# Attention, a mixture of experts and a softplus layer on one core: a staggered front of twelve attention steps, four slots for each later step, and a softplus remainder one slot later

## The chip, the cores and the metric

The kernel runs on one core of one Trainium2 chip. The metric is the device time of one execution in microseconds, the median of some runs. The matmuls are TensorE's (PE in the rows); VectorE (DVE), ScalarE (ACT) and GpSimd (POOL) work beside it, each on its own queue in order, and SyncE (SP) issues most transfers.

## What is computed

```python
# attention: 4 batches, 8 heads, 576 queries, head dimension 64; keys and values are averaged over 8
k_p = k.reshape(B, H, Sp, pool, D).mean(axis=3)
v_p = v.reshape(B, H, Sp, pool, D).mean(axis=3)
scores = scale * np.matmul(q, k_p.transpose(0, 1, 3, 2))
attn = softmax(scores)                       # exp of the scores minus their maximum, over the sum + 1e-9
x = matmul(attn, v_p)                        # as 2304 rows of 512
# mixture of 8 experts, 512 -> 1024 -> 512
P = exp(x @ w_gate - max); 8 times: rows to sum 1, columns to sum 1, times N / E
for e in range(E):
    out += P[:, e:e + 1] * (np.maximum(x @ w1[e], 0.0) @ w2[e])
# softplus layer, 512 -> 2048 -> 512
h = out @ w_in
g = np.maximum(h, 0.0) + np.log1p(np.exp(-np.abs(h)))
y = g @ w_out
```

## The kernel before, in words

**Products.** The 2304 rows are three thirds of 768. A phase is one layer over one third: three phases of experts, then three of softplus (`phases`). A phase has units of 256 hidden columns, 32 in an expert phase and 8 in a softplus phase, 120 in all. Each operand of a product is a rounded part hi and a remainder lo, and a product is three matmuls (`three`, L524). The first product of a unit (`first`, L553) is a Strassen form with seven block products of 6 matmuls, 128x384 each, 42 in all; its inputs are four blocks of x and sums of them (t1 to t4, `t_sums`), each as hi and lo (`splits`), and four sums of the weights (`sums_w1`, L170, and `prep_w1`, L181). The second product (`second`, L600) takes 6 row tiles of 6 matmuls 128x512, 36 in all, and DVE adds each result from its PSUM bank py onto an accumulator g. The order of work is `todo`: first 0, first 1, second 0, first 2, second 1 and so on. After the first product, `pending` holds four activations. `relu` (L540) or `softplus` (L547) writes h as hi on ACT and as lo on DVE; one of them follows the first product and the others follow the row tiles of the second product before.

**Attention.** It has 32 steps of one pair of heads and 288 queries (`attn_step`, L396). A step turns its queries (`channels_first`, bank pq, copied by ACT), computes the scores (`softmax`, L308, bank s), takes the maximum and the difference on DVE into an SBUF tile ex, exp on ACT, sum and reciprocal on DVE and the product on POOL (`divide`, L326), then six transposes (`turn_attn`, bank pa, copied by ACT to aT) and the mix with V (`mix`, bank px, copied by ACT into x or xb). Each fourth step is followed by `gate` (bank pg). Keys and values of a pair of heads are used by eight steps over two halves of the queries. In the front the keys are summed by 16 matmuls with the identity (`keys_first`, bank pk) and the values by three additions on POOL; later two reductions on DVE do it (`pool_kv`, L255) and one transpose.

The first 14 steps (`AHEAD`) run ahead of all products, the front. Then the sums and parts of x for the first third are made (L807 to L817). The other 18 steps run inside the products: `hook` (L749) is called at some 13 slots of a unit, 7 in its first product and 6 in its second, and every fifth slot runs one whole step. When attention has ended, the slots work off the list `side` (the gate's normalisation, the shares of the experts whose sums were kept raw, `shares_to_raw`), and later the conversion of the softplus weights from 64-bit floats (`from_float64`) and the preparation of the next phase's x (`turn`, `t_sums_banked`, `remainders`). Before expert 4 of the first phase `flush` runs what is left in the list at once (L880); the shares of the fourth expert are put there just before (L895).

**PSUM.** While attention runs, all eight banks are one pool. Then they are four for the first product (p), three for py and the side work's banks (xs, xh, pt), and one for the conversion (c).

The order on each engine is the order in which the code is written (`manual_schedule`); tiles wait for the release of the buffer that they take.

## Time and profile before

| | us |
|---|---|
| median of 3 runs (2056.94 to 2063.78) | 2063.13 |
| the profiled execution | 2063.6 |
| its span in the profile | 2061.8 |

| engine | busy us | share | instructions |
|---|---|---|---|
| PE (matmul) | 2010.8 | 98% | 10643 |
| DVE | 1364.5 | 66% | 2417 |
| POOL | 1258.2 | 61% | 1069 |
| ACT | 822.5 | 40% | 1607 |

Matmuls overlap in a pipeline, so their busy time counts some time twice and hides short gaps; the pace of matmuls that follow each other (start to start) tells more. A row of the timeline shows in brackets how long the engine was idle before it and what ended that. PEclk is the granted clock of TensorE as a share of 2.4 GHz; its other level is 1.2 GHz.

### The profile page before, as it was taken

Reading aid. Unit: us, or ns where it says so; the run is one execution under the profiler, and the core shown is the slowest. Engines: PE = TensorE matmul, PEld = TensorE weight load, DVE = VectorE, ACT = ScalarE, POOL = GpSimd, SP = SyncE. Lnnn points to the kernel's source line nnn. Section 1 sums busy time; section 2 is a strip of 40 time slices with the busy share of each in tenths; the row PEclk is TensorE's granted clock in tenths of the full one; section 3 lists DMA queues with packets and bytes.
Section 4 is the critical chain, followed back from the end, with each engine's and each line's share of the span. In section 5 each row is a group of like instructions: output and inputs, shape, how many; then the busy total and the mean of one; then the engine's idle time right before and its main releaser. Section 6 shows DMA issues by size and latency. Waiting matters only on the chain.

```text
span 2061.8 us, 28361 instructions
## 1 busy us (share of the span) xinstructions
PE 2010.8 (98%) x10643; PEld 1788.7 (87%) x10643; DVE 1364.5 (66%) x2417; ACT 822.5 (40%) x1607; POOL 1258.2 (61%) x1069
## 2 busy tenths in 40 slices
PE   8898999999999999999999999999999999999999
PEld 6677889889989988988899898989989998888998
DVE  3677558777666677677777677666777546546455
ACT  3453544323433333433233423333322455654543
POOL 5554556666566567557666666665676555655653
PEclk8799999999999999999999999999999999999999
DMA  6242122223234234323322432233333323433421
GB/s 167 74 122 80 61 75 62 82 92 118 85 114 126 81 92 134 94 92 102 103 98 92 152 113 96 87 89 98 92 103 102 104 79 96 144 93 110 160 63 62
DMA packets 142311, 205.70 MB, mean 100 GB/s; under 512 B 27916, under 2 KB 88796, under 8 KB 142172
## 3 DMA queue, kind: packets, MB, share of 16 engines
q1 hardware_dynamic: 132092, 190.12, 30.1%
q10 hardware_dynamic: 10080, 13.77, 1.8%
q8 instruction: 83, 1.36, 0.3%
q14 instruction: 56, 0.46, 0.1%
HBM read 173.76 MB, written 30.09 MB: 99 GB/s over the span
## 4 chain that ended last, share of the span: by engine, by line
PE 83%; DVE 5%; POOL 5%; ACT 3%; issue 3%; DMA 1%; SPq 0%; ACTq 0%; DVEq 0%; POOLq 0%
PE py L527 41%; PE p L527 37%; POOL w1lo L165 2%; PE s L314 1%; ACT w1hi L194 1%; PE px L352 1%; POOL w2lo L165 1%; PE pk L297 1%; POOL sums L165 1%; PE pa L342 1%; DMA f<-in_moe_w_out_dram 1%; DVE p L569 1%; DVE za L569 0%; PE pq L283 0%; DMA f<-in_moe_w_in_dram 0%
## 5 line engine op out<-in xcount | busy, mean ns | idle before, releaser
L527 PE MATMUL py<-w2hi,hhi 128*128 128x512 f32 x1440 | 565.9, 393 | 15.7 <-DVE g L614 8.9
L165 POOL TENSOR_TENSOR w1lo<-w1raw,w1hi 128x512 fp32r<-128x512 f32 x240 | 241.8, 1029 | 556.1 <-ACT w1hi L194 556.1
L527 PE MATMUL p<-xhi,w1hi 128*128 128x384 f32 x1680 | 568.2, 338 | 10.2 <-DVE p L569 4.6
L527 PE MATMUL p<-xlo,w1hi 128*128 128x384 f32 x1680 | 564.8, 336 | 3.6 <-DVE xlo L479 3.6
L527 PE MATMUL p<-xhi,w1lo 128*128 128x384 f32 x1680 | 565.1, 336 | 3.0 <-POOL w1lo L165 3.0
L527 PE MATMUL py<-w2hi,hlo 128*128 128x512 f32 x1440 | 565.8, 393 | 0.0
L527 PE MATMUL py<-w2lo,hhi 128*128 128x512 f32 x1440 | 565.1, 392 | 0.0
L629 DVE SCALAR_TENSOR_TENSOR g<-py,prob,g 128x512 f32<-128x512 f32 x468 | 349.7, 747 | 94.8 <-PE py L527 83.5
L527 PEld LDWEIGHTS p<-xhi,w1hi 128*128 128x128 f32 x1680 | 316.6, 188 | 28.2 <-DVE p L569 7.5
L527 PEld LDWEIGHTS py<-w2hi,hhi 128*128 128x128 f32 x1440 | 271.1, 188 | 78.4 <-DVE g L614 12.8
L542 ACT ACTIVATE hhi<-p 128x384 fp32r<-128x384 f32 x384 | 180.5, 493 | 391.2 <-PE p L527 347.6
L527 PEld LDWEIGHTS p<-xlo,w1hi 128*128 128x128 f32 x1680 | 316.6, 188 | 14.2 <-DVE xlo L479 4.4
L527 PEld LDWEIGHTS py<-w2hi,hlo 128*128 128x128 f32 x1440 | 270.8, 188 | 57.6
L527 PEld LDWEIGHTS p<-xhi,w1lo 128*128 128x128 f32 x1680 | 316.4, 188 | 3.6 <-POOL w1lo L165 3.6
L527 PEld LDWEIGHTS py<-w2lo,hhi 128*128 128x128 f32 x1440 | 270.9, 188 | 49.0
L165 POOL TENSOR_TENSOR w2lo<-w2raw,w2hi 128x1024 fp32r<-128x1024 f32 x120 | 289.5, 2412 | 14.8 <-ACT w2hi L202 14.8
L165 POOL TENSOR_TENSOR w1lo<-sums,w1hi 128x1024 fp32r<-128x1024 f32 x120 | 289.4, 2411 | 0.0
L571 ACT COPY za<-p 128x384 f32<-128x384 f32 x120 | 57.5, 479 | 538.7 <-PE p L527 538.7
L543 DVE SCALAR_TENSOR_TENSOR hlo<-p,hhi 128x384 fp32r<-128x384 f32 x384 | 210.4, 548 | 28.8 <-ACT hhi L542 28.7
L569 DVE TENSOR_TENSOR za<-p,za 128x384 f32<-128x384 f32 x120 | 66.8, 556 | 215.4 <-PE p L527 215.4
L569 DVE TENSOR_TENSOR u<-p,za 128x384 f32<-128x384 f32 x120 | 66.8, 556 | 126.4 <-PE p L527 92.5
L202 ACT CAST w2hi<-w2raw 128x1024 fp32r<-128x1024 f32 x120 | 126.5, 1054 | 0.0
(111 smaller groups left out, 2015.3 us busy)
## 6 DMA issues: line engine op xcount, KB each, us to landing
w1raw<-in_moe_w_dram SPq DMA_DIRECT2D x96, 512.0 KB
w2raw<-in_moe_w_dram SPq DMA_DIRECT2D x96, 512.0 KB
xlod<-xl ACTq DMA_DIRECT2D x70, 192.0 KB
xlo<-xlod SPq DMA_DIRECT2D x35, 384.0 KB
w1raw<-v SPq DMA_DIRECT2D x24, 512.0 KB
w2raw<-v SPq DMA_DIRECT2D x24, 512.0 KB
f<-in_moe_w_in_dram SPq DMA_DIRECT2D x16, 512.0 KB
v<-dt SPq DMA_DIRECT2D x32, 256.0 KB
```

Source lines behind the costliest of these rows:

```text
L165: nc.gpsimd.tensor_tensor(o, a, b, op=ALU.subtract)
L194: nc.scalar.copy(at(hi), src)
L202: nc.scalar.copy(hi, raw)
L297: nc.tensor.matmul(pk[h * D:(h + 1) * D, :SP], kt[:, h, t, :], ident[:SP, :SP], start=t == 0, stop=t == POOL - 1,)
L314: nc.tensor.matmul(ps[:QP, j * 2 * SP:(j + 1) * 2 * SP], qT[:, j * QP:(j + 1) * QP], kb)
L342: nc.tensor.transpose(pa[:SP, j * QP:(j + 1) * QP], ex[:, 2 * j + h, :], ident[:QP, :QP])
L527: nc.tensor.matmul(ps, lhs[a], rhs[b], start=first and i == 0, stop=last and i == 2, skip_group_check=goes_on,)
L542: nc.scalar.activation(hh, src, AF.Relu)
L543: nc.vector.scalar_tensor_tensor(hl, src, 0.0, hh.bitcast(F32), op0=ALU.max, op1=ALU.subtract)
L569: add = lambda o, x, y: nc.vector.tensor_tensor(o, x, y, op=ALU.add)
L571: nc.scalar.copy(a, pa)
L629: nc.vector.scalar_tensor_tensor(a, py, prob[:, t, e:e + 1], a, op0=ALU.mult, op1=ALU.add)
```

## The change

- **The front** is a loop of 12 steps and two more passes in which each part of a step has its own iteration: `front(k)` runs the scores of step k, the transposes of step k - 2, the queries of step k + 1, exp of step k, the keys for later, the division of step k - 1 and the mix of step k - 2. In these steps the difference and exp are written back into the scores' bank, and the division's product is DVE's, from the bank into ex. The keys' bank is copied by ACT (before: DVE). Values are summed on POOL always.
- **x of the first third**: `mix` also writes hi and lo of b11, b21 and b22 from the bank px (ACT and DVE); t1 to t4 are summed and split in halves inside the front's last iterations, partly on POOL. Unit 0's first product begins inside the last two passes (block products m1 and a12), and units 0 and 1 have their weights prepared inside the front.
- **Each later step** has four slots: queries and scores; exp, the transposes of the step before, the first half of a key reduction; division and values; mix and the second half of the key reduction.
- **The shares of the fourth expert** are put into the list behind the flush.
- **Softplus**: the remainder of each activation is DVE's one entry of `pending` later. In the last phases `turn`, xs and xh take the bank c instead of a py bank.
- `load_kv` loads K and V apart; the numbers in `keys_summed` and `values` load pairs 6 and 7 of both twice.

```diff
+    AHEAD = 12
...
-    AHEAD = 14
...
+    def values(i):
+
+        vt = v_t.pop(i)
         vp = at_p.tile([SP, 2, D], F32, tag="vp", name="vp", bufs=NK + 1)
-        early = pooled_at[i] < AHEAD
-        kp = None
-        if not early:
-            kp = at_p.tile([SP, 2, D], F32, tag="kp", name="kp", bufs=1)
-            nc.vector.tensor_reduce(kp, kt.rearrange("p h t d -> p h d t"), axis=AX.X, op=ALU.add)
-        if early:
-            pool_add(vt[:, :, 0:4, :], vt[:, :, 0:4, :], vt[:, :, 4:8, :])
-            pool_add(vt[:, :, 0:2, :], vt[:, :, 0:2, :], vt[:, :, 2:4, :])
-            pool_add(vp, vt[:, :, 0, :], vt[:, :, 1, :])
-        else:
-            nc.vector.tensor_reduce(vp, vt.rearrange("p h t d -> p h d t"), axis=AX.X, op=ALU.add)
-        pooled[i] = kp, vp
-        if early:
-            keys_first(i, kt)
-
-        if pool is ld_p or next_kv[0] < 2 * HP:
-            load_kv(pool)
+        pool_add(vt[:, :, 0:4, :], vt[:, :, 0:4, :], vt[:, :, 4:8, :])
+        pool_add(vt[:, :, 0:2, :], vt[:, :, 0:2, :], vt[:, :, 2:4, :])
+        pool_add(vp, vt[:, :, 0, :], vt[:, :, 1, :])
+        vp_t[i] = vp
+        load_kv(i + (4 if i < 4 else 2), v_t)
...
+        keys_out(i, pk, lambda o, a, s: nc.scalar.activation(o, a, AF.Copy, scale=s))
+        load_kv(i + (4 if i < 4 else 2), k_t)
...
+    def keys_reduced(i, h):
+
+        if h == 0:
+            kp_t[i] = at_p.tile([SP, 2, D], F32, tag="kp", name="kp", bufs=1)
+        nc.vector.tensor_reduce(
+            kp_t[i][:, h], k_t[i][:, h].rearrange("p t d -> p d t"), axis=AX.X, op=ALU.add
+        )
+        if h:
+            del k_t[i]
+            load_kv(i + 2, k_t)
...
+        ev = sv if early else turned()
         nc.vector.tensor_reduce(mx, sv, axis=AX.X, op=ALU.max)
-        nc.vector.tensor_tensor(ex, sv, mx.unsqueeze(2).to_broadcast([QP, G, SP]), op=ALU.subtract)
+        nc.vector.tensor_tensor(ev, sv, wide(mx), op=ALU.subtract)
         def exp():
-            nc.scalar.activation(ex, ex, AF.Exp)
+            nc.scalar.activation(ev, ev, AF.Exp)
         def divide():
             sm = at_p.tile([QP, G], F32, tag="sm", name="sm")
-            nc.vector.tensor_reduce(s1, ex, axis=AX.X, op=ALU.add)
+            ex = turned() if early else ev
+            nc.vector.tensor_reduce(s1, ev, axis=AX.X, op=ALU.add)
             nc.vector.tensor_scalar_add(s1, s1, 1e-9)
             nc.vector.reciprocal(sm, s1)
-            nc.gpsimd.tensor_tensor(ex, ex, sm.unsqueeze(2).to_broadcast([QP, G, SP]), op=ALU.mult)
+            (nc.vector if early else nc.gpsimd).tensor_tensor(ex, ev, wide(sm), op=ALU.mult)
             to_turn.append((m, ex))
-        return exp, divide
+        to_exp.append(exp)
+        to_divide.append(divide)
...
+        if here:
+            tb = TP0 // 2
+            for j in range(2):
+                a, z = max(t0, j * tb), min(t0 + here, (j + 1) * tb)
+                if a < z and (hp // 2, j) in first_x:
+                    hi, lo = (t[:, hp % 2, a - j * tb:z - j * tb] for t in first_x[hp // 2, j])
+                    src = px[:, a - t0:z - t0]
+                    nc.scalar.activation(hi, src, AF.Copy, scale=1.0 / POOL)
+                    nc.vector.scalar_tensor_tensor(
+                        lo, src, 1.0 / POOL, hi.bitcast(F32), op0=ALU.mult, op1=ALU.subtract
+                    )
...
+    keys_at = {-1: (0,), 0: (1,), 1: (2,), 2: (3,), 4: (4,), 5: (5,), 6: (6,), 7: (7,)}
+    pooled_at = {8: 12, 9: 13, 10: 14, 11: 15, 12: 18, 13: 21, 14: 22, 15: 23}
...
+    def attention():
+        for m in range(AHEAD, STEPS + 2):
+            now = [i for i in pooled_at if pooled_at[i] == m]
+            while to_gate:
+                gate()
+            if m + 1 < STEPS:
+                channels_first(m + 1)
+            if m < STEPS:
+                softmax(m)
+            yield
+            while to_exp:
+                to_exp.pop(0)()
+            while to_turn:
+                turn_attn()
+            for i in pooled_at:
+                if pooled_at[i] == m - 1:
+                    keys_turned(i)
+            for i in now:
+                keys_reduced(i, 0)
+            yield
+            while to_divide:
+                to_divide.pop(0)()
+            for i in now:
+                values(i)
+            yield
+            while to_mix:
+                mix()
+            for i in now:
+                keys_reduced(i, 1)
+            yield
+    def front(k):
+        if k < AHEAD:
+            softmax(k)
+        if to_turn:
+            turn_attn()
+        if k + 1 <= AHEAD:
+            channels_first(k + 1)
+        while to_exp:
+            to_exp.pop(0)()
+        for i in keys_at.get(k, ()):
+            keys_summed(i)
+        while to_divide and (len(to_divide) > 1 or k >= AHEAD):
+            to_divide.pop(0)()
         while to_gate:
             gate()
+        if to_mix:
             mix()
...
-                    got.append(bank("xs")[:, :a.shape[2]])
+                    got.append(bank("xs", spare[0])[:, :a.shape[2]])
...
-        nc.vector.tensor_tensor(hl, src, hh.bitcast(F32), op=ALU.subtract)
+        return lambda: nc.vector.tensor_tensor(hl, src, hh.bitcast(F32), op=ALU.subtract)
...
+            tail = [None]
+            for x, i, j in order:
+                def act(x=x, i=i, j=j):
+                    if tail[0]:
+                        tail[0]()
+                    tail[0] = softplus(at(i, j), ps(x))
+                pending.append(act)
+            pending.append(lambda: tail[0]())
...
+    def first(n, between, done=None):
+        do = done or first_parts(n)
+        order = ("s1", "s2", "a22", "s3") if done else ("m1", "s2", "s1", "a22", "s3", "a12")
+        for k, x in enumerate(order):
+            do[x]()
+            between(k)
...
-        if attn_m[0] is not None:
-            if slot[0] % 5 == 2:
-                attn_step(attn_m[0], False)
-                attn_m[0] += 1
-                if attn_m[0] >= STEPS and not to_turn and not to_mix and not to_gate:
-                    attn_m[0] = None
-                    finish_attention()
+        if attn[0] is not None:
+            if next(attn[0], 0) == 0:
+                attn[0] = None
+                finish_attention()
...
+    def t_half(eng, i, a, b):
+        return lambda c: eng.tensor_tensor(t0_of(i)[:, c], a(c), b(c), op=ALU.subtract)
+    def t_split(eng, name, i, c):
+        if c == 0:
+            xs_next[name] = [xpool.tile([P, 2, TP0 // 2], F32R, tag="x", name=f"x{n}") for n in ("hi", "lo")]
+        hi, lo = (t[:, c] for t in xs_next[name])
+        nc.scalar.copy(hi, t0_of(i)[:, c])
+        eng.tensor_tensor(lo, t0_of(i)[:, c], hi.bitcast(F32), op=ALU.subtract)
+    x0_sum = {
+        1: t_half(nc.gpsimd, 0, on_b(0, 1), on_b(0, 0)),
+        3: t_half(nc.gpsimd, 2, on_b(1, 1), on_b(0, 1)),
+        2: t_half(nc.vector, 1, on_b(1, 1), on_t(0)),
+        4: t_half(nc.vector, 3, on_b(1, 0), on_t(1)),
+    }
+    xs_next.update({"b11": first_x[0, 0], "b21": first_x[1, 0], "b22": first_x[1, 1]})
...
+    for it in range(AHEAD + 2):
+        if it == AHEAD:
+            xs.update(xs_next)
+            unit0 = first_parts(0)
+            unit0["m1"]()
+        if it == AHEAD + 1:
+            unit0["a12"]()
+        front(it)
+        if it in (0, 1, 2, 3, 4, 5):
+            values(it)
+        if it == 2:
+            load_w(2, 0)
+        if it == 4:
             sums_w1(0)
+            parts[0] = w1_parts(0)
+        if it in (5, 6):
+            next(parts[0])
+        if it == 7:
+            values(6)
+            next(parts[0])
+            next(parts[0], None)
             load_w(1, 1)
+        if it == 8:
+            values(7)
+            ta = hpool.tile([P, 2, 2, TP0 // 2], F32, tag="hhi", name="ta")
+            tb = hpool.tile([P, 2, 2, TP0 // 2], F32, tag="hlo", name="tb")
+            t0_of = lambda i: (ta, tb)[i // 2][:, i % 2]
+        if it == 9:
+            sums_w1(1)
+        if it == 10:
+            parts[1] = w1_parts(1)
+            x0_sum[1](0)
+            t_split(nc.gpsimd, "t1", 0, 0)
+        if it == 11:
+            x0_sum[1](1)
+            t_split(nc.gpsimd, "t1", 0, 1)
+            next(parts[1])
+            next(parts[1])
+        if it in (12, 13):
+            c = it - 12
+            x0_sum[2](c)
+            t_split(nc.vector, "t2", 1, c)
+            x0_sum[3](c)
+            x0_sum[4](c)
+            t_split(nc.gpsimd, "t4", 3, c)
+            t_split(nc.vector, "t3", 2, c)
+    next(parts[1])
+    next(parts[1], None)
+    load_w(1, 2)
...
                 flush()
+                shares_to_raw([RAW - 1])
...
-            if f == 0 and u == RAW * UPE - 1:
-                shares_to_raw([RAW - 1])
...
             if f == 2 and u == NU1 - 1:
                 assert converting[0] is None
+                spare[0] = "c"
```

How instructions move, at three places. On DVE in the front, one step before and one after (mx: the maximum; s<-ex and s<-s: the sum; kbd: the keys):

```order
L320 TENSOR_REDUCE mx<-s 96x6
L321 TENSOR_TENSOR ex<-s,mx 96x432
L302 TENSOR_SCALAR kbd_129<-pk 64x72 x2
L328 TENSOR_REDUCE s<-ex 96x6
L329 TENSOR_SCALAR s<-s 96x6
L330 RECIPROCAL sm<-s 96x6
```

```order
L337 TENSOR_REDUCE mx<-s 96x6
L338 TENSOR_TENSOR s<-s,mx 96x432
L346 TENSOR_REDUCE s<-s 96x6
L347 TENSOR_SCALAR s<-s 96x6
L348 RECIPROCAL sm<-s 96x6
L349 TENSOR_TENSOR ex<-s,sm 96x432
L390 SCALAR_TENSOR_TENSOR xlo<-px,xhi 128x288
```

The keys' copy has left DVE; the product ex and a remainder of x from px have come.

On POOL behind the front, where the first products run (sums and w1lo: weights of the first product, w2lo: of the second, ex: the product of the division, vt and vp: the sums of V), before:

```order
L331 TENSOR_TENSOR ex<-ex,sm 96x432 x3
L165 TENSOR_TENSOR w1lo<-w1raw,w1hi 128x512
L165 TENSOR_TENSOR w1lo<-w1raw,w1hi 128x256
L165 TENSOR_TENSOR w1lo<-sums,w1hi 128x1024
L165 TENSOR_TENSOR w2lo<-w2raw,w2hi 128x1024
```

and after:

```order
L886 TENSOR_TENSOR xlo<-tb,xhi 128x384
L165 TENSOR_TENSOR w1lo<-sums,w1hi 128x1024
L349 TENSOR_TENSOR ex<-ex,sm 96x432
L162 TENSOR_TENSOR vt<-vt 72x2x256
L162 TENSOR_TENSOR vt<-vt 72x2x128
L162 TENSOR_TENSOR vp<-vt 72x128
L165 TENSOR_TENSOR w2lo<-w2raw,w2hi 128x1024
```

The sums of V, which were reductions on DVE here, now stand between a step's product and the remainder of the second product's weights.

On DVE in a softplus phase, from the first block sum of a unit on (u, za and the p tiles: block sums, g: the addition from py), before:

```order
L569 TENSOR_TENSOR p_16850<-p_16850,za 128x384
L551 TENSOR_TENSOR hlo<-p_16847,hhi 128x384
L614 TENSOR_TENSOR g_2974<-py,g_2974 128x512
L569 TENSOR_TENSOR p_16849<-p_16849,u_16852 128x384
L551 TENSOR_TENSOR hlo<-p_16848,hhi 128x384
```

and after:

```order
L632 TENSOR_TENSOR pd<-pd,za 128x384
L702 TENSOR_TENSOR g_2931<-py,g_2931 128x512
L632 TENSOR_TENSOR pc<-pc,u_16876 128x384
L608 TENSOR_TENSOR hlo<-pa,hhi 128x384
L702 TENSOR_TENSOR g_2931<-py,g_2931 128x512
```

The first addition from py now stands ahead of the first remainder, and each remainder is one addition later.

## Rows read from the trace of the kernel before

**Rows 1.** Chain of waits in order of time: start us, us, what.

```profile
345.02 6.84 PE py L527 x30
351.86 6.26 PE p L527 x36
```

**Rows 2.** Busy time by stretch, tile p on PE: length, busy (count), PEclk, DMA.

```profile
0.00:88.50 88.50, 3.16 (x7) 0.79 0.52 137
88.50:300.00 211.50, 82.29 (x413) 0.98 0.28 81
```

**Rows 3.** The same view for tile py.

```profile
88.50:300.00 211.50, 77.17 (x310) 0.98 0.28 81
```

**Rows 4.** Chain of waits in the front, one iteration.

```profile
34.58 0.96 PE pa L342 x6
35.54 2.12 PE pk L297 x32
37.66 0.96 PE px L352 x4
38.62 0.67 PE pq L283 x3
39.29 1.44 PE s L314 x6
```

**Rows 5.** Busy time of PE in one stretch of the front, PEclk and DMA share.

```profile
26.80:88.50 61.70, 50.16 (x463) 0.69 0.38 99
```

**Rows 6.** Timeline of PE: start us, us, instructions [idle before <-releaser].

```profile
53.53 0.69 PE L342 MATMUL pa<-ident,ex 96*72 96x96 f32 x6 [3.12 <-POOL ex L331]
```

**Rows 7.** Timeline of DVE, one softmax of the front.

```profile
50.44 0.60 DVE L320 TENSOR_REDUCE mx<-s 96x6 f32<-96x432 f32 x1 [0.19 <-PE s L314]
51.15 0.60 DVE L321 TENSOR_TENSOR ex<-s,mx 96x432 f32<-96x432 f32 x1
...
52.51 0.19 DVE L330 RECIPROCAL sm<-s 96x6 f32<-96x6 f32 x1
```

**Rows 8.** Groups of instructions on POOL: count | busy us, mean ns | idle before.

```profile
L165 POOL TENSOR_TENSOR w2lo<-w2raw,w2hi 128x1024 fp32r<-128x1024 f32 x120 | 289.5, 2412 | 14.8 <-ACT w2hi L202 14.8
...
L331 POOL TENSOR_TENSOR ex<-ex,sm 96x432 f32<-96x432 f32 x32 | 29.7, 930 | 96.7 <-DVE sm L330 55.6 <-ACT w1hi L194 19.5 <-PE p L527 8.4
...
L162 POOL TENSOR_TENSOR vt<-vt 72x512 f32<-72x512 f32 (+1 forms) x20 | 19.9, 994 | 8.6 <-DMA vt<-in_v_dram 7.8
```

**Rows 9.** Timeline of DVE and PE at the first products.

```profile
82.31 3.42 DVE L479 TENSOR_TENSOR xlo<-g,xhi 128x768 fp32r<-128x768 f32 x1
...
85.79 0.69 PE L527 MATMUL p<-xlo,w1hi 128*128 128x384 f32 x1 [3.28 <-DVE xlo L479]
```

**Rows 10.** Timeline of PE and DVE; last, busy time of all engines in one stretch, PEclk.

```profile
108.66 0.65 PE L527 MATMUL p<-xhi,w1lo 128*128 128x384 f32 x1 [1.70 <-POOL w1lo L165]
...
163.20 1.92 DVE L268 TENSOR_REDUCE vp<-vt 72x128 f32<-72x1024 f32 x1
...
166.24 0.44 PE L527 MATMUL p<-xhi,w1hi 128*128 128x384 f32 x1 [3.07 <-DVE p L569]
...
160.00:170.00 10.00, 6.93 (x28) 5.87 (x27) 8.28 (x12) 4.75 (x9) 7.00 (x5) 0.84 0.55 171
```

**Rows 11.** Timeline of DVE and PE at the flush.

```profile
417.18 0.74 DVE L782 SCALAR_TENSOR_TENSOR g<-g,prob,g 128x512 f32<-128x512 f32 x1
...
422.43 5.29 DVE L782 SCALAR_TENSOR_TENSOR g<-g,prob,g 128x512 f32<-128x512 f32 x3
...
428.44 0.50 PE L527 MATMUL py<-w2hi,hhi 128*128 128x512 f32 x1 [2.47 <-DVE g L629]
```

**Rows 12.** Waits of PE in total (us, times, longest), and DVE's timeline.

```profile
PE py L527 <- DVE g L614: 8.9, 8, 1.6
...
PE py L527 <- DVE g L467: 2.3, 2, 1.1
...
1736.46 0.56 DVE L551 TENSOR_TENSOR hlo<-p,hhi 128x384 fp32r<-128x384 f32 x1 [1.03 <-ACT hhi L550]
```

More of the change, by code (lines that the diff above doesn't have):

```diff
@@ L566, in first, with ps @@
         tb = PAIRS[sets[n][2]] // 2
-        pa, pb, pc, pd = (bank(f"p{x}", "p")[:, :tb] for x in "1654")
+        got = {}
+        def ps(x):
+            if x not in got:
+                got[x] = bank(f"p{x}", "p")[:, :tb]
+            return got[x]
         a, u1 = (zpool.tile([P, tb], F32, tag="z", name=x) for x in ("za", "u1"))
         add = lambda o, x, y: nc.vector.tensor_tensor(o, x, y, op=ALU.add)
-        product(pa, A11, "b11")
-        nc.scalar.copy(a, pa)
-        between(0)
-        product(pb, S2, "t2")
@@ L574, in first @@
-        add(u1, pb, a)
-        between(1)
-        product(pc, S1, "t1")
-        between(2)
-        product(pd, A22, "t4")
-        between(3)
-        product(pb, S3, "t3", True)
-        add(a, pb, a)
-        add(pb, pc, a)
-        add(pd, pd, a)
-        between(4)
-        product(pa, A12, "b21", True)
-        between(5)
-        def rest():
-            product(pc, S4, "b22", True)
-            add(pc, pc, u1)
-        between(6)
-        act = relu if sets[n][1] == "moe" else softplus
@@ L594, in first, with m1, s2, s1 @@
-        pending.extend([
-            lambda: act(at(0, 0), pa), lambda: act(at(1, 1), pb),
-            lambda: act(at(1, 0), pd), lambda: act(at(0, 1), pc),
-        ])
-        return rest
+        def m1():
+            product(ps("a"), A11, "b11")
+            nc.scalar.copy(a, ps("a"))
+        def s2():
+            product(ps("b"), S2, "t2")
+            add(u1, ps("b"), a)
+        def s1():
+            product(ps("c"), S1, "t1")
+        def a22():
+            product(ps("d"), A22, "t4")
@@ new lines, in s3, with a12, s4, out @@
+        def s3():
+            product(ps("b"), S3, "t3", True)
+            add(a, ps("b"), a)
+            add(ps("b"), ps("c"), a)
+            add(ps("d"), ps("d"), a)
+        def a12():
+            product(ps("a"), A12, "b21", True)
+        def s4():
+            product(ps("c"), S4, "b22", True)
+            add(ps("c"), ps("c"), u1)
+        def out():
+            order = (("a", 0, 0), ("b", 1, 1), ("d", 1, 0), ("c", 0, 1))
+            if sets[n][1] == "moe":
+                pending.extend([lambda x=x, i=i, j=j: relu(at(i, j), ps(x)) for x, i, j in order])
+                return
+            tail = [None]
[6 more added lines that the diff above has]
+            pending.append(lambda: tail[0]())
@@ L861, in between @@
                 hook()
-            rest = first(n, between)
+            rest = first(n, between, None if n else unit0)
             pending.pop(0)()
```

193 lines of the change are left out of this document (86 added, 107 removed).

## The prediction, made before the run

> **What bounds the kernel now.** I read the trace in this order: the pace of the products, then the product time by stretch, then each stretch that falls short. In an undisturbed stretch 30 matmuls of the second product take 6.84 us and 36 of the first take 6.26 us, 0.228 and 0.174 us each [rows 1]. The reader should see that no wait lies in those rows: PE is the bound there. The program has 120 units with 36 of the one and 42 of the other, 985 + 877 = 1862 us. The other 200 us of the span of 2061.8 us are attention, transposes and lost time, and only these can change.
>
> Where they lie shows in [rows 2, 3]. Before 88.5 us there are 7 products, so 87 us are something else. From 88.5 to 300 us the 413 and 310 recorded products are worth 71.9 + 70.7 = 142.6 us of 211.5, so 69 us are something else. The 44 us that are left lie behind 300 us, a good part of them in two places to which T3 and T4 come.
>
> **The front** (0 to 88.5 us) is PE work at the wrong clock. One iteration of it, without a wait between its pieces, is pa 0.96, pk 2.12, px 0.96, pq 0.67, s 1.44: 6.15 us [rows 4], and 4.03 us where no keys are summed. The granted clock from 26.8 to 88.5 us is 0.69 of full [rows 5]: 38% of that time at 2.4 GHz, the rest at 1.2, and the five rows are at the lower. PE waits there for POOL's product now and then, 3.12 us at the most [rows 6].
>
> **The change, part by part. T1, the front.** The loop runs 12 steps instead of 14; exp runs in the scores' bank, the division is DVE's, and each step's transposes use a product made an iteration earlier. So PE no longer waits for POOL. DVE pays: maximum, difference, sum and two small operations take 2.26 us from 50.44 to 52.70 us [rows 7]. The product from PSUM is not in the trace; its nearest rows are the difference of the same shape (0.60) and POOL's product (0.93) [rows 7, 8]; I take 0.60, since it is the same engine, bank and width. The remainder of b11, b21 or b22 from px is at most 288 wide, against 0.56 for a remainder 384 wide [rows 12]: 0.45. DVE: 3.3 to 3.7 us an iteration. ACT gets the scaled keys (two of about 0.2 us) and one more copy of px (0.4) in place of nothing; at 4 us an iteration it has room, as DVE has. So at 1.2 GHz PE is still the bound, and at 2.4 GHz DVE is, at about 3.6 us.
>
> The loads K, Q, K, Q, V come in an order that PE needs, so I let the scores of step 3 begin at 24.5 us (25.34 before). From there at 1.2 GHz: one iteration without keys, four with, four without, two gates of 1.1, then 12 matmuls of the first product and the last two transposes and mixes: 4.0 + 24.6 + 16.1 + 2.2 + 4.2 + 4.6 = 55.7 us, the end at 80.2. With DVE as the bound: 9 x 3.6 + 4.6 = 37, the end at 61.5. With 38% of the time at 2.4 GHz as before: 55.7 / (1 + 0.5 x 0.38) = 47, the end at 71; I take 74, as the four iterations without keys leave PE idle at full clock. Then 12 mixes are done as at 88.5 us before; two scores and two query transposes fewer (2.1 us at full clock), five products more (0.9): 75.2 in place of 88.5. **T1 = -13 us (-7 to -26).**
>
> SP sends four loads of K and V twice (18 + 18 in place of 16 + 16, 288 KB each); DMA is 0.38 busy there [rows 5], so nothing, or some 2 us in the first iterations if they delay others, which is inside the bounds.
>
> **T2, from the front to the last step.** Before, the first products wait 3.28 us for a remainder of x that takes DVE 3.42 us [rows 9], then 1.70 us and 1.29 us for unit 1's weight remainders on POOL (the longer of them in [rows 10]). Unit 1's weights are now prepared in the front, and x is split as it comes. At 166 us PE waits 3.07 us right after the two pooled reductions of 2 us each on DVE, and 2.70 us the same way at 188 (the first in [rows 10]). The clock falls behind such a stall: 0.84 of full is granted from 160 to 170 us [rows 10], 1.6 us of work lost, and as much behind the stalls at 105 and 108 us. The keys' reduction is now two halves of 1 us in different slots, and V's goes to POOL (vt, vt, vp). Removed: 3.0 + 5.8 + 2 x 1.6 = 12 us; the 3.28 is in T1.
>
> Added: at the junction the t2, t4 and t3 halves follow the last mix. DVE does four operations of 128x384 with both inputs in SBUF, then the scores' maximum and difference, and the fourth product waits for the addition behind them. Clean, at the 0.74 us that 512 columns take [rows 11], these four are 2.2 us; at the pace of the 3.42 us row 6.8. PE meanwhile has one product and a step, 3.6 us, and ACT's copies in the chain take some 1.5. So PE waits 0 to 4.7 us; I take 3, because POOL works beside it all through. What that is worth shows in another place: the addition of 0.74 us, both inputs in SBUF, takes 5.29 us for three beside POOL [rows 11]. The Trainium skill (SBUF — State Buffer, Who interferes with whom) says that a VectorE instruction with two SBUF inputs contends with GpSimd's reads and one with a PSUM input does not. The trace agrees; without it the wait would be nearer 0 and the sum 3 us lower.
>
> POOL is behind once: remainders of unit 1, the sums of V, w2lo 2.41 us [rows 8] and the sums of unit 2 stand in its queue before the product of step 13; I put 2 us of PE's wait there (0 to 6). **T2 = -12 + 3 + 2 = -7 us (0 to -14).**
>
> **T3, the shares.** At 422 us three of them run back to back for 5.29 us, and the next DVE addition frees PE's bank 2.47 us late [rows 11]; the clock falls behind it too, 1.6 us as above. Attention ends after 88 slots in place of about 100, nothing is left to flush, and the last expert's shares get their own slots. **T3 = -4 us (-2.5 to -4.4).**
>
> **T4, the softplus phases.** PE waits 8.9 us in 8 pieces for DVE's additions behind the bank, and 2.3 us for L467 [rows 12]. The row at 1736.46 us is the cause: DVE's remainder waits 1.03 us for ACT's cast, which stands behind weight casts, and the bank's addition stands behind DVE's remainder. One slot later the cast is done. The side work's copies move from the three py banks to the one converting bank, where each waits for the one before; they are two or more slots of 0.8 us apart, and ACT's burst of weight casts is 2 us, so PE's transposes may wait up to 1.4 us a few times. **T4 = -10 us (-3 to -12).**
>
> Sum: -13 - 7 - 4 - 10 = -34. Against the profiled execution's 2063.6 us (the median shown is 0.5 us lower) that is 2029.6, **2030 us**.
>
> **Rivals.**
> *Full clock in the front.* PE has no waits on POOL left there; if the clock stays at 2.4 GHz, T1 is -26 and the time 2017. For it: two of the falls come right after such waits. Against it: from 34.58 to 40.73 us PE is back to back and stays at half [rows 4]. The Trainium skill (TensorE: Matmul & The Clock Gate, Part 1) says that activity releases the throttle; by that rule a front without waits is this rival, and those rows do not agree with it.
> *The front gains nothing*, because PE at 1.2 GHz bounds it as before and the junction takes what two fewer steps give: T1 = 0, 2043.
> *The one bank costs what it frees*: transposes and copies of x queue behind one another, T4 = 0 to +2: 2040 to 2042.
> *Slower: POOL late in each of 20 steps.* From division to transposes there are now three slots, about 5 us (a thirteenth of 15.5 us plus a quarter of a step, three times), and five before. Weight remainders (1.0 + 0.5 + 2.4), w2lo 2.4 and the sums of V (two vt of 0.99 and a smaller vp, 2.4) [rows 8] can stand ahead, 8.7 us, so PE waits up to 3.7 us at pa. At 2.5 us a step this is 50 us: 2080. It decides from 34 / 20 = 1.7 us a step. Against it: POOL has about 18 us of work in the 23 us that a unit with its steps takes, and that queue is full only at the first units.
>
> **Chances.** Forecast 0.50 (2020 to 2041), full clock 0.15, nothing in the front 0.17, one bank 0.08, POOL late 0.10. The range: 2010 to 2052, from most of the gains at their upper bounds to all at their lower; about 0.15 is left out, most of it above. About 0.3%, 6 us, is what a measurement of this kernel can tell from no change. Faster by more: 0.84; within: 0.08, from the weak ends of the front's rival and of POOL's; slower: 0.08.
>
> **What would show it.** T1: PE's first product near 70 us, no wait for POOL's ex before it, DVE near 3.6 us an iteration. T2: no PE wait behind a reduction, one of some 3 us for t4 or behind u. T3: no three L866 rows in a row at about 400 us. T4: no PE wait above 1 us for a py bank between 1660 and 1870 us; instead perhaps pt waits for ACT. Wrong if granted clock or PE's end of the front lies outside 61 to 80 us, or if pa waits for POOL in most late steps.

## The result, and the profile after

| kernel | median us | single times | ratio to before, 95% interval |
|---|---|---|---|
| before | 2062.35 | 2056.94 to 2063.78 (4) | |
| changed | 2028.51 | 2022.24 to 2035.85 (4) | 0.9842 [0.9804, 0.9880] |

The changed kernel is faster by 1.6%. The forecast was 2030 us with a range of 2010 to 2052. The profiled execution took 2028.1 us, its span is 2026.3 against 2061.8.

To see where the 35 us come from, both traces can be laid beside each other by products: each has all 9360 matmuls of the two products, so the n-th of one is compared with the n-th of the other. The table holds start times in us, taken from PE's records; a difference that stays the same from one row to the next means that nothing was gained or lost between them.

| product | what ends there | before | changed | difference |
|---|---|---|---|---|
| 1 | the front, nearly | 81.82 | 64.24 | -17.6 |
| 250 | | 169.18 | 150.73 | -18.5 |
| 750 | attention in the background (ended before) | 304.42 | 286.06 | -18.4 |
| 1250 | | 405.30 | 387.01 | -18.3 |
| 1500 | the fourth expert's shares | 459.67 | 437.54 | -22.1 |
| 7500 | the moe units | 1664.74 | 1644.37 | -20.4 |
| 9000 | the softplus phases with side work | 1984.12 | 1949.19 | -34.9 |
| 9360 | | 2057.16 | 2022.23 | -34.9 |

**The front.** First busy time by stretch: window, its length, busy time (count) of PE, PEld, DVE, ACT and POOL, PEclk, DMA share, GB/s.

```profile
0.00:26.80 26.80, 20.49 (x182) 17.99 (x183) 8.76 (x22) 8.00 (x21) 10.54 (x19) 1.00 0.85 190
26.80:60.00 33.20, 26.57 (x333) 20.00 (x333) 21.98 (x53) 20.37 (x62) 19.54 (x23) 0.90 0.73 186
60.00:74.00 14.00, 10.21 (x47) 7.53 (x46) 7.46 (x19) 8.84 (x28) 7.44 (x8) 0.66 0.10 23
```

Then PE's timeline, cut to the rows that tell the story (start, length, instructions, in brackets the idle time before and what ended it).

```profile
24.08 1.75 PE L326 MATMUL s<-kbd,qT 128*96 128x144 f32 x6
...
31.33 0.98 PE L326 MATMUL s<-kbd,qT 128*96 128x144 f32 x6
...
34.61 0.98 PE L326 MATMUL s<-kbd,qT 128*96 128x144 f32 x6
...
41.87 2.19 PE L283 MATMUL pk<-ident,kt 72*64 72x72 f32 x32 [5.41 <-DMA kt<-in_k_dram]
...
46.23 1.56 PE L326 MATMUL s<-kbd,qT 128*96 128x144 f32 x6
...
63.41 0.90 PE L371 MATMUL px<-aT,vp 72*64 72x288 f32 x4 [1.17 <-ACT aT L362]
...
64.52 0.52 PE L584 MATMUL pa<-xlo,w1hi 128*128 128x384 f32 x1
...
67.95 1.42 PE L371 MATMUL px<-aT,vp 72*64 72x288 f32 x4 [0.67 <-ACT aT L362]
...
74.24 1.43 PE L371 MATMUL px<-aT,vp 72*64 72x288 f32 x4 [1.69 <-ACT aT L362]
...
79.79 0.34 PE L584 MATMUL pb<-xlo,w1hi 128*128 128x384 f32 x1
```

The scores need 1.75 us at 1.2 GHz and 0.98 us at 2.4. From about 27 us on PE runs at 2.4 GHz, and an iteration with keys takes 3.28 us (31.33 to 34.61) where it took 6.15 us before [rows 4]. PE has no idle time in that iteration, and DVE is busy for 2.90 us of it. Then PE waits 5.41 us for the keys of pair 6, and behind this wait it is at 1.2 GHz until 47 us. The last three waits of the front are for ACT's copy of the transposed attention, and from 64.5 to 78 us PE is at 1.2 GHz once more: a product takes 0.52 us there and 0.34 us behind.

The last mix of the front ends at 75.7 us, with 12 products done. In the kernel before, the twelfth mix ended at 80.35 us, but the products ran on only from 88.5 us, behind the sums and remainders of x [rows 9]:

```profile
79.69 0.66 PE L352 MATMUL px<-aT,vp 72*64 72x288 f32 x4
...
88.56 0.69 PE L527 MATMUL p<-xlo,w1hi 128*128 128x384 f32 x1 [0.30 <-DVE xlo L479]
```

So the mix itself ends 4.7 us earlier. The larger part of the gain is that x is split by then: the 8.2 us between the last mix and the products are gone. Of the POOL waits of [rows 6] none is left.

**From 88 to 300 us.** All that PE waits for in this stretch (the waits of 1.0 and 0.6 us between 82 and 86 us come under T2), by engine, line and what it waited for: us in total, times, longest.

```profile
PE py L584 <- DVE kbd L271: 2.2, 1, 2.2
PE pa L584 <- DVE g L713: 0.9, 1, 0.9
PE pb L584 <- DVE hlo L600: 0.6, 1, 0.6
PE pk L304 <- DVE hlo L600: 0.2, 1, 0.2
PE pa L361 <- POOL ex L349: 0.2, 1, 0.2
```

The waits of 3.07 and 1.70 us [rows 10] have gone, and POOL's product is late once, by 0.2 us. The longest wait that is left, 2.2 us, starts from a reduction of keys that itself waits for its load, on DVE:

```profile
166.67 1.08 DVE L294 TENSOR_REDUCE kp<-kt 72x64 f32<-72x512 f32 x1 [1.20 <-DMA kt<-in_k_dram]
```

**The shares.** The six of the fourth expert now stand apart on DVE's timeline (with one row of POOL and one of PE between them).

```profile
405.62 2.41 POOL L165 TENSOR_TENSOR w1lo<-sums,w1hi 128x1024 fp32r<-128x1024 f32 x1
...
406.78 1.80 DVE L866 SCALAR_TENSOR_TENSOR g<-g,prob,g 128x512 f32<-128x512 f32 x1
...
409.29 0.50 PE L584 MATMUL py<-w2hi,hhi 128*128 128x512 f32 x1 [0.26 <-DVE g L717]
...
411.41 0.74 DVE L866 SCALAR_TENSOR_TENSOR g<-g,prob,g 128x512 f32<-128x512 f32 x1
...
413.39 0.74 DVE L866 SCALAR_TENSOR_TENSOR g<-g,prob,g 128x512 f32<-128x512 f32 x1
```

Two of the six, the first and the last, still take 1.8 and 2.1 us, with POOL's weight remainders beside them. Behind the first PE waits 0.26 us; its wait of 2.47 us [rows 11] is gone.

**The softplus phases.** Between 1635 and 1900 us the list of PE's waits is empty; before it held 8.9 and 2.3 us [rows 12]. In all that comes behind 300 us PE waits for this:

```profile
PE pc L584 <- DVE pb L632: 3.1, 5, 1.3
PE py L584 <- DVE g L717: 2.2, 8, 0.3
PE py L584 <- DVE g L713: 0.5, 2, 0.3
```

The 1.8 us given back between products 1500 and 7500 are mostly in the first of these rows (before, waits of this kind held 1.6 us behind 300 us). In the chain of waits DVE is held up at one of these five places by a load of the side conversion, `f`, and PE by DVE:

```profile
914.22 5.61 DMA f<-in_moe_w_out_dram
922.66 2.10 DVE db L800
```

The undisturbed pace is what it was [rows 1]:

```profile
467.63 6.84 PE py L584 x30
```

### The profile page after: what moved, and what is told of

Read it like the earlier page. It is cut to its first block, busy times and chain, and to the rows that moved or that the text cites. A ratio compares the mean times of both kernels' runs of the same rounds, so it can differ in the third digit from the quotient of the medians.

```text
span 2026.3 us, 28308 instructions
## 1 busy us (share of the span) xinstructions
PE 1994.1 (98%) x10581; PEld 1776.5 (88%) x10581; DVE 1358.3 (67%) x2434; ACT 825.0 (41%) x1636; POOL 1260.7 (62%) x1075
## 4 chain that ended last, share of the span: by engine, by line
PE 71%; POOL 3%; issue 2%; DVE 2%; DMA 1%; ACT 1%; ACTq 0%; SPq 0%; POOLq 0%
PE py L584 37%; PE pb L584 10%; PE pa L584 9%; PE pc L584 9%; PE pd L584 5%; POOL w1lo L165 2%; DMA f<-in_moe_w_in_dram 1%; POOL w2lo L165 1%; ACT w1hi L194 1%; DMA f<-in_moe_w_out_dram 0%; POOL sums L165 0%; PE pt L723 0%; ACT hhi L599 0%; DVE za L632 0%; DVE g L717 0%
## 5 line engine op out<-in xcount | busy, mean ns | idle before, releaser
L632 DVE TENSOR_TENSOR za<-pb,za 128x384 f32<-128x384 f32 x120 | 66.7, 556 | 212.5 <-PE pb L584 212.5
L584 PE MATMUL pc<-xhi,w1hi 128*128 128x384 f32 x480 | 162.6, 339 | 3.7 <-DVE pb L632 3.7
L584 PE MATMUL pa<-xhi,w1hi 128*128 128x384 f32 x480 | 163.8, 341 | 0.9 <-DVE g L713 0.9
L584 PE MATMUL pb<-xhi,w1hi 128*128 128x384 f32 x480 | 162.2, 338 | 1.6 <-DVE u L632 1.0
L584 PE MATMUL pa<-xhi,w1lo 128*128 128x384 f32 x480 | 162.6, 339 | 0.0
L584 PE MATMUL pa<-xlo,w1hi 128*128 128x384 f32 x480 | 162.0, 338 | 0.0
L584 PE MATMUL pc<-xlo,w1hi 128*128 128x384 f32 x480 | 161.9, 337 | 0.0
L584 PE MATMUL pc<-xhi,w1lo 128*128 128x384 f32 x480 | 161.2, 336 | 0.0
L584 PE MATMUL pb<-xhi,w1lo 128*128 128x384 f32 x480 | 160.5, 334 | 0.0
L584 PE MATMUL pb<-xlo,w1hi 128*128 128x384 f32 x480 | 160.5, 334 | 0.0
```

The source lines that it names most:

```text
L584: nc.tensor.matmul(ps, lhs[a], rhs[b], start=first and i == 0, stop=last and i == 2, skip_group_check=goes_on,)
L632: add = lambda o, x, y: nc.vector.tensor_tensor(o, x, y, op=ALU.add)
```

## The experiments

Each is the changed kernel with one thing altered, unless said otherwise. Differences are read from the start times of products, as above, since the part that an edit doesn't touch then falls out. In the runs whose edit lies elsewhere, products 1250 to 1500 take 50.5 to 50.6 us and products 7500 to 9000 take 304.8 to 305.2, so for these two stretches a single execution is enough. In the front it is not.

**1. Loads once (nodup).**

```diff
-        load_kv(i + (4 if i < 4 else 2), k_t)
+        if i not in (4, 5):
+            load_kv(i + (4 if i < 4 else 2), k_t)
```

The same for `v_t`.

> The changed kernel, but K and V of pairs 6 and 7 are loaded once (the second issue of each is left out). Theory: in the changed kernel PE waits 5.41 us at 36.5 us for the keys of pair 6 because the tile it uses is the second copy, issued at about 31 us behind other loads; with one copy they are there in time. Then that wait goes, and the half clock right behind it (from 41.9 to 47.6 us) with it: PE's first product begins near 57 us in place of 64.2, and the time falls by 6 to 8 us against the changed kernel, 2021 us. Rival: the DMA engines are full there (0.93 busy from 30 to 40 us), so the keys come late whatever is issued: the wait shrinks to some 3 us at most and the time falls by 0 to 3 us.

Measured: 2017.22 us median of 4 (2016.03 to 2018.89), ratio to before 0.9788 [0.9771, 0.9804]. The first product starts at 56.18 us. PE's waits for keys up to 100 us, first of the changed kernel, then of this one:

```profile
PE pk L283 <- DMA kt<-in_k_dram: 10.1, 2, 5.4
```

```profile
PE pk L284 <- DMA kt<-in_k_dram: 4.6, 1, 4.6
```

What is left is the wait for the very first load. PE sums the keys of pair 6 at 36.33 us, right where it waited in the changed kernel, and its clock does not fall there:

```profile
26.80:45.00 18.20, 17.98 (x263) 13.82 (x262) 15.93 (x38) 15.86 (x48) 11.74 (x15) 1.00 0.63 165
```

The theory holds: the first product is 8.06 us earlier, of which 5.4 us are the wait, and the other 2.6 are what 5.6 us of work at half clock lose (some 2.8). The rival, full DMA engines, falls in the form that it had, since no wait is left. The run also takes the traffic of the second copies away, but the trace of the changed kernel tells the two apart: there the first copy of pair 6, issued at 24.63 us, had landed by 30.0 us, and the wait ends when the second lands. The whole time is 11 us lower than the changed kernel's median and not 8; the next run shows how far single executions spread.

**2. The changed kernel once more (again).** No edit.

> The changed kernel itself once more, unaltered. In the runs with the order of other places altered PE's first product began at 56 to 57 us or at 64 us, with the loads issued alike. Theory (the keys of pair 6 come just in time or just late, as the transfers fall): the single times spread over 8 us or more, about 2018 to 2030 us, and the profiled one has either no wait over 2 us for the keys of pair 6, or one of 4 to 6 us. Rival (the wait is fixed, and the others differ for another reason): a spread of under 4 us and the wait of 5.4 us again.

Measured: 2025.11 us median of 5, single times 2020.92 to 2034.66; in the profiled one the keys of pair 6 cost 2.8 us:

```profile
PE pk L283 <- DMA kt<-in_k_dram: 7.2, 2, 4.4
```

The spread is as the theory says, the wait is neither of the two sizes that it named. Over the ten traces that issue these loads alike (this one, the first one and those below) the wait for pair 6 is 5.4, 5.2, 4.2, 2.9, 2.8, 1.2, 0.9 and three times 0 us. In the seven of them whose front is otherwise that of the changed kernel and whose edit lies elsewhere, the first product starts at 63 to 64 us where the wait is 2.8 us or more (changed, again, oldtail, vdve below) and at 56 to 57 us where it is 1.2 us or less (swap, onekey, ybank). So the second copies, issued at 33.49 us in the changed kernel and needed at 36.46, come just in time or just late, and a late one also costs the clock. The four times with loads once lie within 3 us. Experiments 4 and 8, which load once too, have three later ones, so these loads are not all of the spread.

**3. The product on POOL again (exsbuf, exsbuf2).** exp in SBUF (with a third buffer), the division's product in the front on POOL; the staggered order stays.

```diff
-        ev = sv if early else turned()
+        ev = turned()
-            ex = turned() if early else ev
-            (nc.vector if early else nc.gpsimd).tensor_tensor(ex, ev, wide(sm), op=ALU.mult)
+            ex = ev
+            nc.gpsimd.tensor_tensor(ex, ev, wide(sm), op=ALU.mult)
```

> The changed kernel with exp in SBUF and the softmax's product in the front on POOL, as they were in the kernel before; the staggered order stays. Theory (the clock in the front rose because PE no longer waits for POOL each iteration): PE waits for POOL's ex several times between 27 and 60 us, the granted clock of that stretch falls towards the 0.71 of the kernel before, and PE's first product begins 5 to 12 us later than in the changed kernel. Rival: the product is made an iteration ahead, so POOL has time: no waits for ex, the same clock, the first product within 2 us of that of the changed kernel (56 to 57 us, or 64 where the keys of pair 6 come late).

Measured: 2035.4 us, the first product at 71.27 us, but neither theory holds. PE waits 0.5 us for POOL up to 300 us, and not in the front, and yet it is slow. Its timeline, and the busy time of the stretch (PE alone, then PEclk, DMA share, GB/s):

```profile
28.22 1.76 PE L326 MATMUL s<-kbd,qT 128*96 128x144 f32 x6
...
54.31 1.75 PE L326 MATMUL s<-kbd,qT 128*96 128x144 f32 x6
...
67.63 0.98 PE L326 MATMUL s<-kbd,qT 128*96 128x144 f32 x6
```

```profile
27.00:60.00 33.00, 33.00 (x266) 1.00 0.53 146
```

PE is busy without a gap from 24 to 66 us, and every matmul takes the time of 1.2 GHz. The column PEclk says 1.00 there, as it does for the first 26.8 us of the kernel before, where the durations are also those of 1.2 GHz: the record begins with the first change, so durations decide.

> Once more the changed kernel with exp in SBUF and the front's product on POOL, unaltered, now with several times. In the first look PE waited for POOL's ex for 0.5 us in all, and yet PE ran back to back at half speed from 24 to 66 us (the scores 1.75 us in place of 0.98). Two theories. One: the half speed is a draw of the single execution, which the changed kernel's own late runs (2034 to 2036 us) show too; then most times here are 2018 to 2030 us and one in five or so lies near 2035 us. The other: with the product on POOL the clock does not rise in the front; then all times lie between 2031 and 2038 us and the profile shows the scores at 1.75 us up to some 60 us again.

Measured: 2025.49 to 2032.03 us in five executions, median 2030.20. In the profiled one the clock rose by 23 us and PE waited for POOL:

```profile
PE pa L361 <- POOL ex L349: 5.9, 3, 2.8
```

So the half speed of the first trace is not fixed by the edit: it differs between executions of one kernel. The median is 3 us above that of all nine times of the changed kernel (2027.3), with ranges that overlap, so these runs do not show that POOL in the front costs anything; it does not cost the 15 us of the first trace. Why the clock stayed down in that one, with PE back to back, stays open.

**4. The junction's order (hoist, both).** The transposes of the last two front steps are issued ahead of the casts of the halves t1 to t4.

```diff
             unit0 = first_parts(0)
+            turn_attn()
             unit0["m1"]()
...
         front(it)
+        if it == AHEAD:
+            turn_attn()
```

The two splits of t1 move an iteration later, too.

> The changed kernel with the order at the junction altered: the transposes of the last two front steps (and ACT's copies of them) are issued ahead of the casts of the halves of t1 to t4, which wait for POOL's and DVE's sums. Theory: PE's waits for ACT's aT copies (excess of 1.3, 0.9 and 2.0 us between 62 and 74 us) come from ACT's queue, where the casts stand in front; without them 4 us go, and if the granted clock stays full from 62 to 79 us another 3 to 5: time 2020 to 2024 us. Rival: DVE's chain of sums and remainders of the halves ends last; then PE waits later, for t4 or behind u, for as much as it saved, and the time is within 2 us of the changed kernel's 2028.5.

Measured: 2023.83 us median of 4, and in the profile, up to 100 us:

```profile
PE pg L404 <- ACT xb L381: 2.1, 1, 2.1
...
PE pb L584 <- DVE u L632: 1.4, 1, 1.4
```

The waits for aT are gone, 3.5 us. These two rows stand in their place, 2.1 us new and 1.0 grown to 1.4. Here the keys of pair 6 were 5.2 us late, too. At product 250 the profiled execution is level with the changed kernel (+0.2 us), with a first product 3.7 us later (six transposes now stand ahead of it, and PE was at half clock from 38 to 62 us). So both theories hold in part: the queue of ACT was the cause of those waits, and two thirds of what it cost reappear later in the chain of the halves.

> Loads once and the junction's order altered, together. If both theories hold the gains add up: 2013 to 2017 us. If DVE's chain of halves is what ends last, this is the time of the loads alone, about 2021 us; if the DMA engines bound the front, that of the order alone.

Measured: 2017.17 us median of 4, with 2016.09 in the profile. The gains do not add up: against loads once the trace is 2.8 us shorter, and the median is the same; one of the four times is 2031.93. In the profiled execution the clock stays full through the junction, where it was at half in the changed kernel and with loads once (PEclk 0.66 and 0.63 in the same stretch):

```profile
60.00:74.00 14.00, 8.68 (x76) 6.50 (x76) 11.30 (x19) 8.09 (x20) 8.56 (x7) 1.00 0.23 64
```

At product 19 it is 7.5 us ahead of loads once, at product 1250 2.5. Why the rest is lost between them stays open.

**5. The shares in a row (swap).**

```diff
-                flush()
                 shares_to_raw([RAW - 1])
+                flush()
```

> The changed kernel, but the last expert's shares are queued ahead of the flush, so that they run back to back as in the kernel before. Theory (T3): three additions of 128x512 with both inputs in SBUF in a row, 4.4 to 5.3 us beside POOL, and PE waits 1.5 to 2.6 us once for a py bank, with a fall of the clock behind it: 3 to 4.5 us lost near 400 us. Rival (the earlier end of attention gave T3's gain, not the place of the shares): under 1 us lost.

Measured: between products 1250 and 1500 it loses 9.2 us against the changed kernel, twice what was expected, since all six shares now run in a row and not three:

```profile
395.33 9.93 DVE L866 SCALAR_TENSOR_TENSOR g<-g,prob,g 128x512 f32<-128x512 f32 x6
```

```profile
405.98 0.80 PE L584 MATMUL py<-w2hi,hhi 128*128 128x512 f32 x1 [8.16 <-DVE g L717]
```

The theory holds: 1.65 us a share, near the 1.76 of [rows 11], all in front of the addition that frees PE's bank. Attention ends as early here as in the changed kernel, so its earlier end alone does not give the gain.

**6. Keys and values in a piece (onekey, vdve).** In onekey both halves of a pair's keys are reduced in one slot; vdve has that and V's reduction on DVE behind them.

```diff
             for i in now:
                 keys_reduced(i, 0)
+                keys_reduced(i, 1)
+                values(i, True)          # vdve alone: one reduction on DVE
             yield
```

> The changed kernel, but both halves of a late pair's keys are reduced in the same slot, 2.1 us of DVE in a piece, for the 8 late pairs. Theory (T2: the reduction in a piece makes the additions behind it late): PE waits 1 to 3 us for an addition (u, pb, g) behind a reduction at two or more of the 8 places, and the clock falls behind one or two; 4 to 8 us lost between 80 and 200 us. Rival (it was V's reduction on DVE, which stood behind the keys', that made PE wait; 2.1 us alone are covered): under 2 us lost.

Measured: from product 19 to 750 it takes 204.4 us, the changed kernel 206.5 and 205.8 in its two traces. In six other traces with the same late steps it is 203.3 to 205.5. Halving the keys gains nothing that these tell from nothing.

> The changed kernel, but a late pair's keys and values are both reduced on DVE in one slot, as in the kernel before, some 4 us of DVE in a piece. Both halves of the keys in one slot cost nothing. Theory (V's move to POOL is what took T2's waits away): PE waits 2 to 3 us for u, pb or g behind these reductions at two or more of the 8 places, the clock falls behind them, and 4 to 8 us are lost between 80 and 200 us. Rival (the waits of the kernel before came of its five slots' order): under 2 us.

Measured: 215.5 us for the same products, 9 us more. The waits between 64 and 260 us:

```profile
PE pa L364 <- POOL ex L352: 5.2, 6, 2.2
...
PE pc L585 <- DVE pb L633: 3.4, 1, 3.4
```

So of the two edits to the late pairs, V's move is the one that counts. vdve puts V both on DVE and right behind the keys; V on DVE in a slot of its own was not run, so the engine and the place are not told apart. That the additions behind the reductions come late is only a part of it, since PE waits longer in sum for POOL's product, whose divisor stands behind the reductions, too.

**7. The softplus phases (oldtail, ybank).** In oldtail the remainder stands behind its cast again, in ybank the side work's copies stay in the three py banks.

```diff
-            tail = [None]
-            ...
+                pending.append(lambda x=x, i=i, j=j: softplus(at(i, j), ps(x))())
```

```diff
-                spare[0] = "c"
```

> The changed kernel, but the softplus remainder stands right behind its cast in the same slot, as in the kernel before; the side work's copies stay in the converting bank. Theory (T4's sentence: DVE's remainder waits for ACT's cast behind the weight casts, and the addition that frees the py bank stands behind the remainder): PE's waits for py from DVE's additions come back in the softplus phases, in about 8 places of 0.7 to 1.7 us, and the stretch from 1650 to 1870 us loses 8 to 12 us more than in the changed kernel. Rival (the copies in the py banks made PE wait, the remainder only stood beside them): it loses less than 3 us.

> The changed kernel, but the copies and transposes of the side work stay in the three py banks in the softplus phases; the remainder stays a slot later. If the remainder's place was the cause: 1 to 4 us lost, PE's waits for DVE's subtraction of copies (two, 1.1 us) come back and little else. If the bank was the cause: 8 us or more are lost in the stretch from 1650 to 1870 us.

| from product 7500 to 9000 | us | above the changed kernel |
|---|---|---|
| changed | 304.8 | |
| oldtail | 310.5 | 5.7 |
| ybank | 310.9 | 6.1 |
| before | 319.4 | 14.6 |

The waits between 1635 and 1900 us, of oldtail and then of ybank:

```profile
PE py L584 <- DVE g L697: 3.7, 6, 1.4
```

```profile
PE py L584 <- DVE g L524: 2.3, 2, 1.1
PE py L584 <- DVE g L702: 1.4, 6, 0.3
```

Both expectations are wrong in size. The remainder alone costs 5.7 us and not 8 to 12, the bank alone 6.1 and not 1 to 4, and the kernel before, which has both in their old places, loses 2.8 us more than the sum of the two. A late remainder may matter more while copies also hold py banks; no run shows it. The start-to-start times also show more than the list of waits does (3.7 us in either): the gap in starts is some 0.16 us longer than the wait that is listed, and the matmul behind it is slow by 0.1.

**8. What was best (best).** Loads once, the junction's order, both halves of the keys in one slot.

> Loads once, the junction's order altered, and both halves of a late pair's keys in one slot. By the three runs alone: 2014 to 2017 us, no wait for the keys of pair 6 in the profile, and single times within 4 us of one another (but for a run that is late as a whole). If the second loads are not what makes the front's time spread, the spread stays at 8 us.

Measured: 2016.14 us median of 6, ratio to before 0.9796 [0.9771, 0.9820]; no wait for pair 6. Four times lie between 2014.2 and 2016.7, one is 2024.9 and one 2031.3, and `both` had one of 2031.9. So the expected spread of 4 us was missed, and what makes these late is not the second loads. A front that stays at 1.2 GHz as in the exsbuf trace, 15 us later at the first product than loads once, would give the two late by 15 us, but none of these late executions was profiled. Against loads once alone the median is 1 us lower, which these runs cannot tell from nothing. Loads once beats both kernels; the rest is not shown to add to it.

## Why the prediction was right, and where it was not

The sum was -34 us, and the profiled executions show -35. By terms:

| term | forecast | measured | by |
|---|---|---|---|
| T1, the front | -13 (-7 to -26) | -11.6 | last mix's end at 75.7 us, plus the working's 1.2 for unequal work, against 88.5 |
| T2, to attention's end | -7 (0 to -14) | -6.7 | the rest of -18.3 at product 1250 |
| T3, the shares | -4 (-2.5 to -4.4) | -3.8 | products 1250 to 1500 |
| T4, softplus | -10 (-3 to -12) | -14.6 | products 7500 to 9000 |
| elsewhere | 0 | +1.8 | products 1500 to 7500; mostly DVE, at one place behind a load of `f` |

**T1** has the right size by errors that cancel: the working put the last mix's end at 74 us, and it came at 75.7. The first error is the clock. The working took 38% of the front at 2.4 GHz, "as before"; in the profiled execution PE is at 2.4 GHz from 27 us to the wait, and with loads once the last mix ends at 67.1 us. That is the rival with the full clock, in part; the rival in which the front gains nothing is refuted. At 2.4 GHz the working had DVE as the bound, at about 3.6 us an iteration. An iteration with keys took 3.28 us, with PE busy throughout and DVE for 2.90, so PE is the bound there still (in two iterations without keys PE waits 0.8 and 0.5 us for DVE's product). DVE's two new operations were priced right (0.60 and 0.45 us, measured 0.60 and 0.46).

Against this stands the step on the loads: two more each of K and V were costed at "nothing, or some 2 us". They cost 8.06 us up to the first product (experiment 1), because the tile that is used is the second copy. The DMA share of 0.38 that the step rested on [rows 5] was of the kernel before; with the front running faster the stretch from 26.8 to 60 us has 0.73. Not foreseen either were 3.5 us of waits for aT ahead of the last mix, since casts of the halves that wait for POOL's sums stand in ACT's queue ahead of the copies of aT (hoist).

The claim that PE at 1.2 GHz bounds the front was right for executions in which the clock stays down, as exsbuf shows (6.2 us an iteration with keys, from 28.22 to 34.43 us and on). The reason that was given for a rising clock, no waits for POOL, is not shown: with POOL back the clock was up early in one trace and late in the other. No run takes the front's order or the early split of x back alone, so T1's cause is read from the traces.

The rule that the full-clock rival took from the Trainium skill (TensorE: Matmul & The Clock Gate, Part 1) is that activity releases the throttle. Twelve of the thirteen traces of kernels with this order have the clock up by 28 us, which goes with it; the exsbuf trace, 42 us back to back at 1.2 GHz, does not.

**T2.** Its removal is right, but for another reason than was given in one part: the keys' halves gain nothing (onekey), V's move does (vdve, 9 us). At the junction 3 us of waiting were forecast for t4 or behind u. Measured are 1.0 us for u and 0.6 each for pb and hlo, 2.2 us. The two rows of DVE at the junction agree with the Trainium skill (SBUF — State Buffer, Who interferes with whom), by which a VectorE instruction with two SBUF inputs contends with a GpSimd instruction that reads SBUF: a remainder of the same shape takes 0.56 us alone and 1.04 beside POOL.

```profile
71.81 0.56 DVE L886 TENSOR_TENSOR xlo<-ta,xhi 128x384 fp32r<-128x384 f32 x1 [0.58 <-ACT xhi L885]
...
73.46 0.99 POOL L886 TENSOR_TENSOR xlo<-tb,xhi 128x384 fp32r<-128x384 f32 x1 [2.64 <-ACT xhi L885]
73.83 1.04 DVE L886 TENSOR_TENSOR xlo<-tb,xhi 128x384 fp32r<-128x384 f32 x1 [0.99 <-ACT xhi L885]
```

POOL late for step 13, put at 2 us, was 0.2, and the slower rival, POOL late in each of 20 steps, did not come.

**T3** was right in size and cause (swap, with six shares in a row where the kernel before had three).

**T4** was mis-sized, and the measured value lies outside its bounds. The term was read from the list of waits, 8.9 + 2.3 us, less something. That list leaves out what a stop costs besides the wait, some 0.3 us for each of the ten; by start-to-start times the kernel before loses 14.6 us there against the changed one. The bank was put down as a possible cost, and it is worth 6 us (ybank). The rival "one bank costs what it frees" is refuted.

## What to carry to other kernels

Where two loads of the same tile are issued, the one that is used may be the later, so count not what the extra bytes cost but when the copy that is read is issued; here a wait of 2.8 us for it put the first product 7.0 us later than with loads once, with a fall of PE's clock behind it. A price for a stretch is better taken from start-to-start times against the undisturbed pace than from the list of waits, which held 11.2 of 14.6 us. A kernel whose front depends on a load that is just in time can have times that spread, so one trace of it does not stand for all.

## What the runs showed of the hardware that was not expected

PE can run back to back for 42 us at 1.2 GHz (exsbuf, 24 to 66 us, scores 1.75 us each), while in another execution of the same kernel it is at 2.4 GHz by 23 us. The granted clock in the profile does not show the first such stretch (1.00 for both); the durations do. In the seven traces of experiment 2 a wait of 2.8 us or more for the keys of pair 6 went with a fall of the clock, and one of 1.2 us or less did not. Shorter waits did not always leave it up: at the junction of the changed kernel waits of 0.8, 0.5 and 1.2 us between 57 and 64 us stand ahead of the fall at 64.5.
